# Second layers three turns behind, one split a turn, stores issued later on the sync queue, and the last two half slots under a condition

## The chip, the cores and the metric

The kernel runs on one core of a Trainium2 chip. Its engines work side by side, each in the order of its own instructions: PE (matmuls, with PEld for its weight loads), DVE and ACT (elementwise work; both read PSUM), POOL (small elementwise work, gathers and scatters) and SP, which here only issues DMAs; a DMA at the head of SP's queue that must wait holds all that stand behind it. The metric is the device time of one execution in microseconds (us), the median over runs.

## The reference

```python
X = np.fft.rfft(x, axis=1); y = np.fft.irfft(X * (filt_r + 1j * filt_i), n=3072, axis=1)   # x: 8 x 3072 x 256
h = y.reshape(24576, 256) @ w_in                      # 24576 x 1024
sm = softmax(h); solu = h * sm
ln = (solu - mean) / sqrt(var + 1e-6) * g_ln
z = ln @ w_out                                        # 24576 x 256
logits = cosine(z, expert_emb) / tau                  # 8 experts
e = argmax(logits); gate = softmax(logits)[e]
out = gate * (relu(z @ w1[e]) @ w2[e])                # one expert for each token
```

## The kernel before

The length 3072 is split as 64 x 48, and the transforms become matmuls. Four pairs of batches are worked on, p = 0 to 3. `fft(p)` has two passes: `stage1` loads the input, multiplies and stores to the DRAM tensor `bufA`; the second pass loads `bufA`, transforms over 48, applies the filter and stores to `bufC`. `inv4` takes the last inverse step from `bufC` and leaves tokens, split in two float16 parts (`xh`, L715 and L716), as weights for the first layer.

**Stage B** (`stage_b`) has 192 turns, one for 128 tokens (48 for each p). In turn i PE does the first layer of tile i + 1 (`mm1`, L728, PSUM tile `h`, two buffers), DVE its maximum (`nm`, L893), ACT the exponent (`es`, L929), DVE the product (L930). The second layer (`o`, 24 matmuls, L945) needs `es` transposed and split in a high and a low float16 part, `T`. There are two ways to it. `turn` (L899 to 908) transposes on PE into the tile's `h`, then ACT and DVE split (L907, L908), and only then is that `h` buffer free. `send` (L910 to 917) splits in SBUF (ACT L914, DVE L915, tile `hl`) and lets a DMA of the sync queue transpose (L917). Up to turn 144 the even tiles go by `turn` and the odd ones by `send`; both stand in the odd turn i: `turn(i - 1)` at its start, `send(i)` after the second layer's matmuls. The even turn has neither. The second layer runs LAG = 2 turns behind. `b_final` works out experts, gates and places of each group of 8 tiles, some steps a turn.

Between these pieces `aux` advances the transforms of the next pair (and, for p = 3, the split of the experts' weights, `w_split`), so that in turns 0 to 143 they fill the same engines; their PSUM tiles and inv4's are `a`, two buffers in turn. DMAs on SP stand where the code emits them: the stores of `bufA` (L516) and `bufC` (L679) right behind the ACT instruction that fills their source, the filter load `ft` (L555) inside the first half of a step, the stores of token rows to `xs` (L978) right behind DVE's L974.

**Stage C** (`stage_c`) runs the experts over slots of tokens of one expert: 24 slots of 256 made early, 65 more of 256, and `rest` = 21 half slots of 128, a number that holds for any routing:

```python
full = -(-(n - E * (BLK - 1)) // BLK)          # 89 for n = 24576
rest = (n - full * BLK - E) // 128 + E         # 21
```

A half slot gathers its rows (L1121), has them transposed by DMA (L1126), does 48 matmuls of the first layer (L1197) and 24 of the second (L1160) and scatters 128 rows to `out` (L164). Half slots beyond the last token have ids out of bounds: they do all this and write nothing. The loop is straight code; the instruction stream has no branch in it.

Of the kernel before, what the change touches and what calls it, by code (L numbers as in the profile page):

```python
# [33 lines left out]
LAG = 2  # L34
# [4 lines left out]
WAIT = 4  # L39
MAGIC = 0x5F3759DF  # L40
# [112 lines left out]
class Build:  # L153
    def __init__(self, tc, a, np_run=NP):
        self.tc, self.nc, self.a = tc, tc.nc, a
        self.np_run = np_run
        self.scattered = {}
        self.ld1 = {}
        self.later = []

# [248 lines left out]
    def w_max(self, sp, ps):  # L409
# [5 lines left out]
        for t in range(64 + 2):  # L415
# [81 lines left out]
    def stage1(self, p, part, ap, ps, bufA):  # L497
# [5 lines left out]
        for c in range(n):  # L503
# [5 lines left out]
            for j in range(0, CH, b):  # L509
# [3 lines left out]
                nc.scalar.activation(ao[:, j:j + b, :], t, AF.Copy)  # L513
                yield
            for h in range(2):
                (nc.sync if p else nc.scalar).dma_start(bufA[part, h, c * CH:(c + 1) * CH, :, :].rearrange("n k d -> k n d"), ao[h * 64:(h + 1) * 64])  # L516
# [7 lines left out]
    def fft(self, p, ap, ps, hp):  # L524
# [71 lines left out]
        if p > 0:  # L596
            yield
            yield
            yield
# [16 lines left out]
        for j in range(n + 2):  # L616
            steps = filt(j - 1) if 1 <= j <= n else iter(())
            next(steps, 0)
            if j < n:
# [9 lines left out]
                for i in range(0, KC, b):  # L629
# [8 lines left out]
                    if i == 0:  # L638
                        load2(j + (4 if p > 0 else 2))
                        load_f(j + 2)  # L640
# [16 lines left out]
            for _ in steps:  # L657
                pass
            if j >= n:
                self.load1(p + 1, j - n, ap)  # L660
            if j >= 2:
# [3 lines left out]
                for i in range(0, KC, b):  # L665
# [8 lines left out]
                    nc.scalar.activation(co[:, i:i + b, :], t[:96], AF.Copy)  # L674
                    next(other, 0)
                    yield
                nc.scalar.activation(y[-1], co, AF.Square, accum_out=self.csq[:, p, j - 2:j - 1])
                for h in range(2):
                    (nc.sync if p else nc.scalar).dma_start(bufC[h, first(j - 2):first(j - 2) + KC, :, cols(j - 2)].rearrange("k n d -> n k d"), co[h * 48:(h + 1) * 48])  # L679

        if p > 0:
            yield
            yield
# [56 lines left out]
    def b_final(self, t, p, n2, gw, ps, snap, slow):  # L740
# [74 lines left out]
        if not slow:  # L815
            v.tensor_reduce(gate, pe, axis=AX.X, op=ALU.add)
        yield 2
# [39 lines left out]
    def stage_b(self, xp, bps, gp, ps, hp, op, aux, early):  # L857
# [18 lines left out]
        rows, half = None, None  # L876
# [33 lines left out]
        def send(i):  # L910
# [4 lines left out]
            nc.vector.tensor_tensor(hl[:, 1, :], M["s"], hl[:, 0, :], op=ALU.subtract)  # L915
            T = M["T"] = M["pool"].tile([128, 16, 128], F16, name="T", tag="T")
# [4 lines left out]
        for i in range(n + LAG):  # L921
            j = i - LAG
            now = 0 <= i < n
            if 0 <= i - 1 < n and i != n - 1 and (i % 2 or i > n - N2):
                turn(i - 1)
# [23 lines left out]
            if now:  # L949
                if i % 2 and i < n - N2:  # L950
                    send(i)
# [12 lines left out]
            if now:  # L964
                aux(*divmod(i, N2), 1)
            if 0 <= j < n:
# [4 lines left out]
                def half(j=j, k=k, o=o, c2=c2, rows=rows):  # L971
# [3 lines left out]
                    if k % 2 == 1:  # L975
# [15 lines left out]
        if half:  # L991
            half()
        while finals:
# [14 lines left out]
    def table(self, sp, tp, ps, nb, start, K, blk, out):  # L1008
# [20 lines left out]
        out["taken"] = taken  # L1029
        yield  # L1030
# [64 lines left out]
    def other_slots(self, sp, tp, ps):  # L1095
# [16 lines left out]
        yield from self.table(sp, tp, ps, nb, x2, rest, 128, {})  # L1112
# [16 lines left out]
    def stage_c(self, cb, hp, op, ps, side):  # L1129

        nc = self.nc
        wt = {}

        def load(s):
            while s >= len(self.tables):
                if next(side, 1) == 1:
                    return
            for _ in self.load_slot(s, cb):
# [28 lines left out]

        weights(0, 0)
# [3 lines left out]
        s = 0  # L1172
        late = None
        while s in self.loaded:
            load(s + 2)
            xT = self.loaded.pop(s)
            tab, k = self.tables[s]
            w1, w2 = wt[s]
            n = tab["nh"] * 128
            w1 = w1.rearrange("p (l k f) -> p l k f", l=2, k=2)  # L1180
            w2 = w2.rearrange("p (l k f) -> p l k f", l=2, k=8)
            m = 512 // n
            fs = 1024 // n
            hh, hl = [], []
            for j in range(8 // m):
                if j == 8 // m - 2:
                    weights(s + 1, 0)
                if m * j % fs == 0:
                    hh.append(cb.tile([128, fs, n], F16, name="chh", tag="chh", bufs=2))
                    hl.append(cb.tile([128, fs, n], F16, name="chl", tag="chl", bufs=2))  # L1190
                t = (ps.tile([128, m, n], F32, name="a", tag="a") if j % 2 else hp.tile([128, m, n], F32, name="h", tag="h"))
                for i in range(m):
                    f = m * j + i
                    q = 0
                    for db in range(2):
                        for l, r in ((0, 0), (1, 0), (0, 2)):
                            nc.tensor.matmul(t[:, i, :], w1[:, l, db, f * 128:(f + 1) * 128], xT[:, r + db, :n], start=q == 0, stop=q == 5)  # L1197
                            q += 1
                sl = slice(m * j % fs, m * j % fs + m)
                nc.scalar.activation(hh[-1][:, sl, :], t, AF.Relu)  # L1200
                nc.vector.scalar_tensor_tensor(hl[-1][:, sl, :], t, 0.0, hh[-1][:, sl, :], op0=ALU.max, op1=ALU.subtract)  # L1201
                next(side, 0)
            if late:
                second(late)
            weights(s + 1, 1)
# [148 lines left out]
```

## Time and profile before

| | |
|---|---|
| median of 3 runs | 2778.83 us (2777.41 to 2781.04) |
| the profiled execution | 2770.33 us, its span 2768.5 us, mean granted clock 0.983 |
| first transform alone | 0 to 179 us |
| stage B | 179 to 1698 us |
| stage C | 1698 us to the end |

The page's slices show PE at nine tenths or more nearly everywhere after the first. Matmuls are pipelined and the page models their ends, so a busy PE can hide short gaps; an idle time of a microsecond or more is real. The DMA engines are at seven to nine tenths up to about 1300 us and at three tenths in stage C.

### The profile page before, as it was taken

How to read it: one execution, taken by the hardware profiler on the slowest of the kernel's cores; microseconds unless marked ns; L12 is line 12 of the kernel's file. 1: busy time of each engine (PE TensorE's matmuls, PEld its weight loads, DVE VectorE, ACT ScalarE, POOL GpSimd, SP SyncE). 2: the span in 40 equal slices, each digit the busy share in tenths (PEclk: the TensorE clock that was granted, in tenths of full speed). 3: DMA queues.
4: the chain of work that ended last, by engine and by line, in shares of the span. 5: the costliest groups of instructions: out<-in, count | busy, mean ns of one | idle time of the engine just before them, and what ended most of it. 6: DMA issues, size and time to landing. Idle time of an engine off the chain costs nothing.

```text
span 2768.5 us, 53941 instructions
## 1 busy us (share of the span) xinstructions
PE 2642.6 (95%) x20234; PEld 2035.6 (74%) x20234; DVE 1897.8 (69%) x2976; ACT 1529.8 (55%) x2858; POOL 1245.2 (45%) x2633
## 2 busy tenths in 40 slices
PE   6889999999999998999999998999999999999998
PEld 5447666666666675666677777888888888888898
DVE  5846888867898768988788985554544545545465
ACT  3556777767777766877788864323333333333332
POOL 2001245434555444554455556744454444544444
PEclk8999999999999999999999999999999999999999
DMA  9868888799787798876444432332222333223222
GB/s 316 221 178 248 196 209 185 186 218 211 178 196 181 204 231 201 187 172 140 104 123 121 120 72 50 78 77 73 77 77 75 78 75 78 76 75 79 75 59 57
DMA packets 445398, 384.66 MB, mean 139 GB/s; under 512 B 285995, under 2 KB 368053, under 8 KB 442064
## 3 DMA queue, kind: packets, MB, share of 16 engines
q1 hardware_dynamic: 392288, 310.60, 46.6%
q0 software_dynamic: 27088, 57.48, 6.8%
q10 hardware_dynamic: 25760, 13.14, 1.8%
q8 instruction: 159, 2.61, 0.4%
q14 instruction: 103, 0.84, 0.1%
HBM read 195.93 MB, written 103.35 MB: 108 GB/s over the span
## 4 chain that ended last, share of the span: by engine, by line
PE 30%; issue 23%; POOL 19%; DVE 14%; DMA 8%; ACT 4%; SPq 1%; POOLq 0%; ACTq 0%; DVEq 0%
PE h L728 10%; PE o L945 9%; POOL crow L1121 7%; POOL out_dram L164 6%; POOL scr L163 3%; DVE nm L893 3%; DVE es L930 2%; PE a L512 2%; PE h L904 2%; PE a L667 2%; PE a L710 2%; DMA bufA<-out 2%; DMA c<-bufC 1%; DVE T L908 1%; ACT hl L914 1%
## 5 line engine op out<-in xcount | busy, mean ns | idle before, releaser
L945 PE MATMUL o<-wo_h,T 128*128 128x264 f16 x3072 | 552.8, 277 | 3.3 <-DMA T<-hl 3.2
L1160 PE MATMUL o<-cw,chh 128*128 128x256 f16 x3184 | 527.6, 273 | 0.0
L728 PE MATMUL h<-win_h,xh 128*128 128x512 f16 x1536 | 497.3, 385 | 25.8 <-DVE T L908 22.5
L1197 PEld LDWEIGHTS <-cw 128*128 128x128 f16 x5280 | 476.1, 98 | 57.3 <-POOL gu L761 6.5
L945 PEld LDWEIGHTS <-T 128*128 128x128 f16 x4608 | 452.4, 98 | 70.0 <-DMA T<-hl 3.6
L896 POOL TENSOR_SCALAR gcc<-nm 128x1 f32<-128x1 f32 x192 | 118.6, 618 | 813.3 <-DVE nm L894 533.6
L728 PEld LDWEIGHTS <-xh 128*128 128x128 f16 x2304 | 223.6, 99 | 310.3 <-issue 81.2
L1160 PE MATMUL o<-cw,chl 128*128 128x256 f16 x1592 | 434.0, 273 | 3.0 <-DVE chl L1201 3.0
L945 PE MATMUL o<-wo_l,T 128*128 128x264 f16 x1536 | 425.5, 277 | 0.0
L164 POOL DMA_INDIRECT out_dram<-cot,ids x199 | 218.4, 1097 | 454.8 <-ACT cot L1163 443.0
L1201 DVE SCALAR_TENSOR_TENSOR chl<-h,chh 128x512 f16<-128x512 f32 x199 | 135.8, 683 | 392.1 <-ACT chh L1200 392.1
L1160 PEld LDWEIGHTS <-chh 128*128 128x128 f16 x3184 | 310.6, 98 | 35.5
L1163 ACT ACTIVATE cot<-o,fac 128x256 f32<-128x256 f32 x199 | 94.5, 475 | 423.8 <-PE o L1160 421.8
L1149 DVE COPY cw<-wexp 128x4096 f16 x220 | 279.9, 1280 | 44.3 <-PE o L1160 23.6
L893 DVE TENSOR_REDUCE nm<-h 128x1 f32<-128x1024 f32 x192 | 234.0, 1219 | 105.5 <-PE h L728 105.3
L1197 PE MATMUL h<-cxT,cw 128*128 128x256 f16 (+1 forms) x2640 | 295.1, 263 | 6.8 <-POOL gu L761 6.2
L728 PE MATMUL h<-win_l,xh 128*128 128x512 f16 x768 | 295.9, 385 | 0.0
L1197 PE MATMUL a<-cxT,cw 128*128 128x256 f16 (+1 forms) x2640 | 294.0, 262 | 0.0
L930 DVE SCALAR_TENSOR_TENSOR es<-h,gcc,es 128x1024 f32<-128x1024 f32 x192 | 245.6, 1279 | 65.3 <-ACT es L929 49.4
L929 ACT ACTIVATE es<-h,nm,isc_h 128x1024 f32<-128x1024 f32 x192 | 230.7, 1201 | 61.6 <-DVE nm L894 46.0
L1121 POOL DMA_INDIRECT crow<-xs,ids x199 | 203.5, 1022 | 65.8 <-issue 63.8
L164 POOL DMA_INDIRECT lst<-gdi,gix x192 | 209.1, 1089 | 35.1 <-issue 32.9
(262 smaller groups left out, 4355.9 us busy)
## 6 DMA issues: line engine op xcount, KB each, us to landing
wst<-in_w_dram SPq DMA_DIRECT2D x128, 256.0 KB
in<-in_x_dram SPq DMA_DIRECT2D x48, 512.0 KB
in<-bufA SPq DMA_DIRECT2D x64, 384.0 KB
c<-bufC SPq DMA_DIRECT2D x96, 256.0 KB
xs<-rows SPq DMA_DIRECT2D x96, 256.0 KB
ft<-in_filt_dram SPq DMA_DIRECT2D x24, 960.0 KB
bufA<-out SPq DMA_DIRECT2D x72, 256.0 KB
zw<-z SPq DMA_DIRECT2D x96, 192.0 KB
```

The costliest lines, as they stand in the source:

```text
L164: ins = self.nc.gpsimd.indirect_dma_start(in_offset=None, **kw).ins
L728: nc.tensor.matmul(h[:, nb, :], l[:, i, db, :], r[:, db, sl], start=k == 0, stop=k == 5)
L893: nc.vector.tensor_reduce(x[:, 0:1], L["h"], axis=AX.X, op=ALU.max, negate=True)
L896: nc.gpsimd.tensor_scalar(cc, nm, nm, 1.0, op0=ALU.mult, op1=ALU.max)
L929: nc.scalar.activation(L["s"], L["h"], AF.Exp, bias=L["nm"], scale=self.isc_h[:, i // N2:i // N2 + 1], accum_out=col(i, "st", 0))
L930: nc.vector.scalar_tensor_tensor(L["s"], L["h"], col(i, "cc", 0), L["s"], op0=ALU.mult, op1=ALU.mult, accum_out=col(i, "st", 1))
L945: nc.tensor.matmul(o[:, :D + E], T[:, l, :], r[:, f, :], start=q == 0, stop=q == 23)
L1121: nc.gpsimd.indirect_dma_start(out=rows[:, h, :], out_offset=None, in_=self.xs, in_offset=bass.IndirectOffsetOnAxis(ap=tab["ids"][:, h, k: ...
L1149: nc.vector.tensor_copy(w.rearrange("p (o k) -> p o k", o=1), self.wexp[:, bass.ds(e, 1), part * 4096:(part + 1) * 4096])
L1160: nc.tensor.matmul(o[:, :D], l[f // fs][:, f % fs, h * 128:(h + 1) * 128], w2[:, r, f, :], start=q == 0, stop=q == 23)
L1197: nc.tensor.matmul(t[:, i, :], w1[:, l, db, f * 128:(f + 1) * 128], xT[:, r + db, :n], start=q == 0, stop=q == 5)
L1201: nc.vector.scalar_tensor_tensor(hl[-1][:, sl, :], t, 0.0, hh[-1][:, sl, :], op0=ALU.max, op1=ALU.subtract)
```

## The change

Seven edits in one:

- LAG goes from 2 to 3; `T` has four buffers.
- `send` is cut in two. The split (ACT and DVE) of the odd tile i - 1 stands at the start of the even turn i; the DMA transpose (`post`) follows in that turn behind the second layer's matmuls.
- The stores to `bufA` and `bufC` on the sync queue (p > 0) are held and issued after a later ACT copy (`flush`); the store of token rows (`puts`) is issued at the end of the turn.
- The filter load for p > 0 is issued after the step's filter work rather than in its middle.
- The reduction of `w_max` is emitted one step earlier.
- In the slow form of `b_final` a step is one turn longer.
- The number of half slots in use is read into a register of every engine, and the last two half slots stand in a branch that is taken only if more than 19 are used. The slot loop becomes the function `slots`.

Two tiles that held constants for the first transform move to another pool.

```diff
-LAG = 2
+LAG = 3
+SPARE = 2
@@ w_max
-            yield
             if t >= 2:
                 nc.vector.tensor_reduce(acc[:, (t - 2) // 32, ...
+            yield
@@ stage1 (the same with bufC in fft, where j - 2 is bound too)
                 nc.scalar.activation(ao[:, j:j + b, :], t, AF.Copy)
+                self.flush()
                 yield
-            for h in range(2):
-                (nc.sync if p else nc.scalar).dma_start(bufA[part, h, ...
+            def put(c=c, ao=ao):
+                for h in range(2):
+                    (nc.sync if p else nc.scalar).dma_start(bufA[part, h, ...
+            if p:
+                self.held.append(put)
+            else:
+                put()
+    def flush(self):
+        for f in self.held:
+            f()
+        self.held.clear()
@@ fft
                     if i == 0:
+                        self.flush()
                         load2(j + (4 if p > 0 else 2))
-                        load_f(j + 2)
+                        if p == 0:
+                            load_f(j + 2)
...
             for _ in steps:
                 pass
+            if p > 0:
+                load_f(j + 2)
@@ b_final, after goh
         if not slow:
             v.tensor_reduce(gate, pe, axis=AX.X, op=ALU.add)
+        else:
+            yield
@@ stage_b
+            M["hl"] = hl
+        def post(i):
+            M = live[i]
+            hl = M["hl"]
             T = M["T"] = M["pool"].tile([128, 16, 128], F16, name="T", tag="T")
             nc.sync.dma_start_transpose(out=T, in_=hl.rearrange("p a b -> p (a b)"))
...
-            if 0 <= i - 1 < n and i != n - 1 and (i % 2 or i > n - N2):
-                turn(i - 1)
+            if 0 <= i - 1 < n and i != n - 1:
+                (turn if i % 2 or i > n - N2 else send)(i - 1)
...
             if now:
-                if i % 2 and i < n - N2:
-                    send(i)
+                if 0 < i <= n - N2 and i % 2 == 0:
+                    post(i - 1)
...
                 aux(*divmod(i, N2), 1)
+            if puts:
+                puts.pop()()
...
-                    if k % 2 == 1:
+                    def put():
                         ...
                         nc.sync.dma_start(to[:, nn:nn + 2, :], rows)
+                    if k % 2 == 1:
+                        puts.append(put)
...
-            if i >= n - N2 + SPLIT + 2:
+            if i >= n - N2 + SPLIT + LAG:
                 next(early, 0)
@@ table
+        used = out["used"] = tp.tile([1, 1], I32, name=f"used{len(self.tables)}")
+        v.tensor_copy(used, src[0:1, E - 1:E])
@@ stage_c (the loop over slots is now slots(s), its body as before)
+        stop[0] = end - SPARE                     # load(s) returns for s >= stop[0]
         weights(0, 0)
         next(side)
         load(1)
         weights(0, 1)
+        slots(0)
+        used = nc.values_load(self.used[0:1, 0:1], min_val=0, max_val=end)
+        with tc.If(used > rest - SPARE):
+            stop[0] = end
+            for s in range(end - SPARE, end):
+                load(s)
+            weights(end - SPARE, 0)
+            weights(end - SPARE, 1)
+            slots(end - SPARE)
@@ run
-            bps[0] = ... {"nm": 2, "es": 2, "jk": 1, "hl": 2, "T": 3}
+            bps[0] = ... {"nm": 2, "es": 2, "jk": 1, "hl": 2, "T": 4}
-                    self.m1 += [pp.tile([128, 4, 128], F32, name=f"m1_{k}") for k in range(2)]
+                    self.m1 += [ap.tile([128, 4, 128], F32, name="mt", tag="mt", bufs=3) for _ in range(2)]
```

DVE, in a pair of turns of a second pass. `T` is the split of `turn`, `hl` that of `send`, `es` the product, `xh` inv4's low part, `nm` the maximum of the next tile, `in`, `zw` and `y` the transform. Before, an odd turn and the start of the even one:

```order
L908 TENSOR_TENSOR T<-h,T 128x1024
L930 SCALAR_TENSOR_TENSOR es,gst<-h,gcc,es 128x1024
L974 SCALAR_TENSOR_TENSOR rows<-o,gcc,rows 128x256
L915 TENSOR_TENSOR hl<-es,hl 128x1024
L893 TENSOR_REDUCE nm<-h 128x1
L894 TENSOR_SCALAR nm<-nm,isc_h 128x1
L584 TENSOR_TENSOR y<-z,ft 96x1024
L422 TENSOR_REDUCE wm_a<-wst 128x1
L967 COPY graw<-o 128x8
L792 RECIPROCAL grn<-gnrm 128x8
L930 SCALAR_TENSOR_TENSOR es,gst<-h,gcc,es 128x1024
L716 SCALAR_TENSOR_TENSOR xh<-a,ysc,xh 128x512
```

The same place after the change:

```order
L940 TENSOR_TENSOR T<-h,T 128x1024
L968 SCALAR_TENSOR_TENSOR es,gst<-h,gcc,es 128x1024
L1014 SCALAR_TENSOR_TENSOR rows<-o,gcc,rows 128x256
L925 TENSOR_REDUCE nm<-h 128x1
L926 TENSOR_SCALAR nm<-nm,isc_h 128x1
L600 TENSOR_TENSOR y<-z,ft 96x1024
L423 TENSOR_REDUCE wm_a<-wst 128x1
L1007 COPY graw<-o 128x8
L947 TENSOR_TENSOR hl<-es,hl 128x1024
L968 SCALAR_TENSOR_TENSOR es,gst<-h,gcc,es 128x1024
L746 SCALAR_TENSOR_TENSOR xh<-a,ysc,xh 128x512
```

`hl` has left the place ahead of the maximum `nm` in the odd turn and stands ahead of `es` and `xh` in the even one.

SP, some turns of the same pass. Before:

```order
L650 DMA zw<-z 48x1024
L651 DMA zw<-z 48x1024
L917 DMA_TRANSPOSE T<-hl 128x16x128
L679 DMA bufC<-out 48x4x256 x2
L561 DMA in<-bufA 96x1024
L555 DMA ft<-in_filt_dram 96x2560
L418 DMA wst<-in_w_dram 128x512
L697 DMA mt_8065<-in_m_dram 128x256
L699 DMA c_8067<-bufC 128x512
L978 DMA xs<-rows 128x512
```

After:

```order
L1018 DMA xs<-rows 128x512
L727 DMA mt_8026<-in_m_dram 128x256
L729 DMA c_8028<-bufC 128x512
L955 DMA_TRANSPOSE T<-hl 128x16x128
L669 DMA zw<-z 48x1024
L670 DMA zw<-z 48x1024
L571 DMA ft<-in_filt_dram 96x2560
L703 DMA bufC<-out 48x4x256 x2
L577 DMA in<-bufA 96x1024
L420 DMA wst<-in_w_dram 128x512
```

The transpose stood ahead of the loads of inv4 (`mt`, `c`); it now follows them, and the row store stands ahead of them.

POOL, the end of the program after the change; before, the scatters of `out` run on to the last instruction:

```order
L165 MEMSET scr 1x1
L166 DMA out_dram<-cot,ids_22010 24576x256
L1274 TENSOR_LOAD used_21658
L1275 COMPARE_AND_BRANCH
L1169 DMA crow<-xs,ids_22010 128x256 x2
L165 MEMSET scr 1x1
L166 DMA out_dram<-cot,ids_22010 24576x256
L165 MEMSET scr 1x1
L166 DMA out_dram<-cot,ids_22010 24576x256
L1275 UNCONDITIONAL_BRANCH
L1275 ISA
L1275 UNCONDITIONAL_BRANCH
```

The two half slots stand behind the compare, and the ISA row belongs to the path that leaves them out.

## Rows read from the trace of the kernel before

**Rows 1.** Busy time by stretch: stretch, length, engines' busy time (instructions), clock, DMA share, GB/s.

```profile
700.00:900.00 200.00, 192.13 (x1210) 126.13 (x1210) 181.34 (x284) 155.27 (x294) 106.97 (x255) 0.99 0.81 186
...
179.00:1698.00 1519.00, 1457.66 (x9623) 1006.70 (x9623) 1241.88 (x2122) 1115.73 (x2122) 693.89 (x1920) 0.99 0.71 171
```

**Rows 2.** PE's waits from 179 to 1330: us in total, times, longest.

```profile
PE h L728 <- DVE T L908: 16.5, 10, 3.7
PE a L710 <- DMA c<-bufC: 6.7, 4, 3.0
PE a L633 <- DVE xh L716: 4.9, 3, 1.9
PE a L512 <- DVE xh L716: 3.9, 2, 2.0
PE a L667 <- DVE xh L716: 3.5, 5, 1.4
...
PE o L945 <- DMA T<-hl: 3.2, 2, 2.8
PE a L512 <- ACT hl L914: 2.0, 1, 2.0
```

**Rows 3.** PE's waits from 1330 to 1698.

```profile
PE h L728 <- DVE T L908: 6.0, 6, 1.3
```

**Rows 4.** POOL in order of time, the end: start, us, instruction, idle before.

```profile
2740.64 1.73 POOL L164 DMA_INDIRECT out_dram<-cot,ids  x1 [2.20 <-ACT cot L1163]
...
2745.93 1.73 POOL L164 DMA_INDIRECT out_dram<-cot,ids  x1 [2.20 <-ACT cot L1163]
...
2759.57 0.98 POOL L164 DMA_INDIRECT out_dram<-cot,ids  x1 [1.61 <-ACT cot L1163]
```

**Rows 5.** POOL's DMA queue, 2751.4 to 2756.7 and from 2756.7: packets, MB.

```profile
q0 software_dynamic: 48, 0.04, 2.5%
...
q0 software_dynamic: 96, 0.00, 0.5%
```

**Rows 6.** Lines L1147 and L1350: instructions, ns min/median/max, first and last start.

```profile
L1147 DVEq TENSOR_LOAD <-er x220: 299/307/707, 1698.7 to 2748.9; - x110
...
L1350 POOLq DRAIN  x3: 46/103/8405, 2759.3 to 2768.3; - x3
```

**Rows 7.** DMA queues: an instruction queue; scatters, median us from issue to landing.

```profile
q8 instruction: 159, 2.61, 0.4%
...
out_dram<-cot,ids POOLq DMA_INDIRECT x199, 2.5
```

**Rows 8.** DVE by line, 179 to 1698: busy us, mean ns, idle before.

```profile
L915 DVE TENSOR_TENSOR hl<-es,hl 128x1024 f16<-128x1024 f32 x72 | 88.1, 1223 | 43.3 <-ACT hl L914 43.3
```

**Rows 9.** SP's waits from 179 to 1330.

```profile
SPq L917 <- DVE hl L915: 308.2, 56, 9.9
...
SPq L555 <- DVE zw L590: 49.9, 11, 7.1
```

**Rows 10.** SP and PE in order of time around 1040.

```profile
1035.99 0.95 SPq L555 DMA_DIRECT2D ft<-in_filt_dram  x1
...
1047.03 1.27 PE L710 MATMUL a<-mt,c 128*128 128x128 f32 x8 [2.95 <-DMA c<-bufC]
```

**Rows 11.** DVE and PE in order of time, an even turn.

```profile
1081.95 0.74 DVE L716 SCALAR_TENSOR_TENSOR xh<-a,ysc,xh 128x512 f16<-128x512 f32 x1
...
1084.16 0.58 PE L633 MATMUL a<-hi,d2h 96*96 96x512 f32 x1
```

**Rows 12.** Busy time by stretch behind three gaps of PE.

```profile
391.50:396.00 4.50, 4.33 (x24) 3.08 (x25) 3.92 (x6) 1.62 (x3) 0.28 (x2) 0.62 1.01 345
...
1047.50:1051.50 4.00, 4.00 (x23) 2.95 (x23) 3.25 (x5) 3.68 (x7) 1.31 (x4) 0.57 1.22 218
...
1093.30:1099.50 6.20, 6.17 (x14) 2.38 (x14) 5.89 (x7) 3.30 (x7) 4.85 (x9) 0.53 0.60 132
```

**Rows 13.** The chain that ended last, in order of time.

```profile
197.12 2.70 PE o L945 x24
```

More of the change, by code (lines that the diff above doesn't have):

```diff
@@ L677, in fft, with put @@
                 nc.scalar.activation(y[-1], co, AF.Square, accum_out=self.csq[:, p, j - 2:j - 1])
[L678 to L679 removed]
+                def put(j=j - 2, co=co):
+                    for h in range(2):
+                        (nc.sync if p else nc.scalar).dma_start(bufC[h, first(j):first(j) + KC, :, cols(j)].rearrange("k n d -> n k d"), co[h * 48:(h + 1) * 48])
+                if p:
+                    self.held.append(put)
+                else:
+                    put()
         if p > 0:
             yield
+            self.flush()
             yield
@@ L875, in stage_b @@
         xs = [next(src)]
-        rows, half = None, None
+        rows, half, puts = None, None, []
         def begin(i):
@@ L992, in stage_b @@
             half()
+            puts.pop()()
         while finals:
@@ L1111, in other_slots @@
         yield
-        yield from self.table(sp, tp, ps, nb, x2, rest, 128, {})
+        t2 = {}
+        yield from self.table(sp, tp, ps, nb, x2, rest, 128, t2)
+        self.used = t2["used"]
     def load_slot(self, s, pool):
@@ L1137, in load @@
                     return
+            if stop[0] is not None and s >= stop[0]:
+                return
             for _ in self.load_slot(s, cb):
@@ L1166, in second, with slots @@
                 next(side, 0)
+        def slots(s):
+            late = None
+            while s in self.loaded:
+                load(s + 2)
+                xT = self.loaded.pop(s)
+                tab, k = self.tables[s]
+                w1, w2 = wt[s]
+                n = tab["nh"] * 128
+                w1 = w1.rearrange("p (l k f) -> p l k f", l=2, k=2)
+                w2 = w2.rearrange("p (l k f) -> p l k f", l=2, k=8)
+                m = 512 // n
+                fs = 1024 // n
+                hh, hl = [], []
+                for j in range(8 // m):
+                    if j == 8 // m - 2:
+                        weights(s + 1, 0)
+                    if m * j % fs == 0:
+                        hh.append(cb.tile([128, fs, n], F16, name="chh", tag="chh", bufs=2))
+                        hl.append(cb.tile([128, fs, n], F16, name="chl", tag="chl", bufs=2))
+                    t = (ps.tile([128, m, n], F32, name="a", tag="a") if j % 2 else hp.tile([128, m, n], F32, name="h", tag="h"))
+                    for i in range(m):
+                        f = m * j + i
+                        q = 0
+                        for db in range(2):
+                            for l, r in ((0, 0), (1, 0), (0, 2)):
+                                nc.tensor.matmul(t[:, i, :], w1[:, l, db, f * 128:(f + 1) * 128], xT[:, r + db, :n], start=q == 0, stop=q == 5)
+                                q += 1
+                    sl = slice(m * j % fs, m * j % fs + m)
+                    nc.scalar.activation(hh[-1][:, sl, :], t, AF.Relu)
+                    nc.vector.scalar_tensor_tensor(hl[-1][:, sl, :], t, 0.0, hh[-1][:, sl, :], op0=ALU.max, op1=ALU.subtract)
+                    next(side, 0)
+                if late:
+                    second(late)
+                weights(s + 1, 1)
+                late = (tab, k, w2, hh, hl, fs)
+                if tab["nh"] > 1:
+                    second(late)
+                    late = None
+                wt.pop(s)
+                s += 1
+            if late:
+                second(late)
+        n = self.np_run * 2 * S
+        full = -(-(n - E * (BLK - 1)) // BLK)
+        rest = (n - full * BLK - E) // 128 + E
+        end = full + rest
+        stop[0] = end - SPARE
         weights(0, 0)
@@ L1171, in stage_c @@
         weights(0, 1)
[L1172 to L1205, printed above, removed]
-            late = (tab, k, w2, hh, hl, fs)
-            if tab["nh"] > 1:
-                second(late)
-                late = None
-            wt.pop(s)
-            s += 1
-        if late:
-            second(late)
+        slots(0)
+        assert len(self.tables) == end
+        used = nc.values_load(self.used[0:1, 0:1], min_val=0, max_val=end)
[6 more added lines that the diff above has]
+            slots(end - SPARE)
     def run(self):
```

13 lines of the change are left out of this document (9 added, 4 removed).

## The prediction

> **What bounds the kernel now.** I read the busy times by stretch first, then who PE waited for, then SP's waits, then the last twenty microseconds engine by engine. The stretches [rows 1] should show two regimes. Stage B is 1519.00 us long and PE is busy in 1457.66 of them, so 61.3 us at most are idle; in 700 to 900, where the transforms' second pass fills DVE too, PE has 192.13 of 200 and DVE 181.34. So B is bound by PE with DVE close behind, and no reordering can give more than the idle 61 us plus what the lower clock costs. Stage C has PE without a gap, and only work left out can shorten it.
>
> The waits of PE tell what the 61 us are. Up to turn 144 [rows 2] the largest is the first layer waiting for DVE's T (the buffer `h` that `turn` must leave): 16.5 us in 10 waits. Then come loads from DRAM, `c` 6.7 us, the PSUM buffer `a` that DVE's `xh` must free (4.9 + 3.9 + 3.5 = 12.3 us), the transposed T by DMA 3.2 us, and ACT's `hl` 2.0 us. In the last 48 turns [rows 3], where all tiles go by `turn`, 6.0 us of waits for T are left; nothing of the change moves the split there.
>
> **The two half slots.** Near the end the scatters come 5.29 us apart [rows 4]: that is one half slot, first layer, second layer and no gap. Are the last two in use? The last scatters moved 0.00 MB in 96 packets, and the one before them 0.04 MB in 48 [rows 5]. So 19 of 21 half slots hold tokens; the condition asks for more than 19, and the branch is not taken. The slots end in the same pattern as before (first layer, the second layer of the slot before, the own second layer), two earlier: -2 x 5.29 = -10.6 us, with no cover to lose, since PE is the bound there.
>
> What the condition adds stands at the end of each engine's queue, and POOL is the last. It loads a register: 0.307 us, the median of DVE's loads of an expert's number [rows 6]. Then it waits for its scatters to land, 2.5 us after the issue [rows 7], before the drain may start; before, the drain of 8.405 us began at 2759.3 while the last scatter was still to be issued. From below the cost is the register load, +0.3 us. From above the drain starts at 2759.57 + 2.5 + 0.3 = 2762.4, 3.1 us late. No row shows a compare. I take +2.0, nearer the late drain, since the order puts the wait ahead of it; nothing else is queued there.
> The Trainium skill (Runtime: NRT & Kernel Launch, Instruction fetch mechanics) says that a taken branch whose target is outside the pages held forces a fetch by DMA before the engine goes on. What such a fetch would cost is in the trace: 159 instruction packets take 0.4% of 16 engines' 2768.5 us, 1.1 us each [rows 7]. No run here shows a branch in the stream; that case is a rival below.
>
> **The split in two.** The instructions stay 72 on ACT and 72 on DVE at 1223 ns [rows 8]; they change place. Before, SP stood at the transpose with 308.2 us of waits for DVE's `hl` in 56 turns, the longest 9.9 us, and what was queued behind it (row stores, `in`, `ft`, `c`) waited along; at `ft` it stood another 49.9 us for the filter's `zw` [rows 9]. After, the transpose is issued when its source has been split for most of a turn, and `ft` after its wait is over. I cost SP's freedom only by the waits of PE that it can end.
> - T by DMA: issued earlier in its turn and read as many turns later, it has landed. -3.2 us (bounds 0 and -3.2).
> - `c`: one of the long waits has `ft` issued at 1035.99, the load behind it, and PE idle for 2.95 us before L710 starts at 1047.03 [rows 10]. Here the filter load is a pass's first, which the change leaves where it is, but the held stores ahead of it no longer keep it late. Half of 6.7: -3 us (bounds 0 and -6.7).
> - T by `turn`, 16.5 us: in the odd turn DVE has 1.22 us less to do ahead of the maximum, so the next exponent, and with it the next `es`, comes earlier. In the even turn it has 1.22 us more ahead of `xh` and of everything up to the next T. DVE's sum over the pair is the same, and at nine tenths it leaves little slack. I take a third, -5 us; bounds -16.5 and, where the even turn's delay reaches T, the third rival's price.
> - ACT's `hl`, which held an `a` tile for 2.0 us behind the product that it waited for, now has its source ready at the turn's start: -2.0 us (bounds 0 and -2.0).
> - `a` freed by `xh`: 0. In the turn shown `xh` ends at 1082.69 and PE comes for the third `a` at 1084.16 [rows 11]: 1.47 us of slack, 0.25 after a delay of 1.22.
>
> **The clock.** After such gaps the granted clock falls to its lower level, 1.2 of 2.4 GHz, for a while: 0.62, 0.57 and 0.53 in three stretches with 4.33, 4.00 and 6.17 us of PE work [rows 12]. At full clock these 14.5 us would take little over half; all three gone would be -7 us, and I take -4, the first and half of the others (bounds 0 and -7).
>
> **One turn more of lag.** The 192 second layers stay; one moves from turn 2 to a turn behind the last first layer. There it lies bare: 2.70 us [rows 13]. At the start turn 2 lacks those 2.70 us, but its end is set by the chain through ACT and DVE, which the matmuls had covered in part. Between 0 and +2.7: +1.5 us. The step that `b_final` gains, the earlier reduction and the copy of the count lie on DVE and POOL beside PE's work and are taken at 0, a few tenths a group if DVE has no room.
>
> **The sum.** -10.6 + 2.0 - 3.2 - 3 - 5 - 2 - 4 + 1.5 = -24.3 us. The profiled execution took 2770.33 us, 1.83 more than its span, and would come to 2746.0. The median of the timed runs is 8.50 us above it; what is saved is work and waits, not a share, so I carry the difference: 2778.83 - 24.3 = 2754.5 us.
>
> **The rivals.**
> - Stage C alone: SP's waits go, but PE's are set by DVE and by transfers that compete for the DMA engines whatever the order. For it: DVE at 181.34 of 200, and half of `c`'s waits lie where `ft` is under way. Against it: the T by DMA waits on nothing else. -10.6 + 2.0 + 1.5 = -7.1: 2771.7 us.
> - All of it: the odd turn's relief frees T in time everywhere, and the clock holds. -10.6 + 0.3 - 3.2 - 6.7 - 16.5 - 2 - 7 + 0 = -45.7: 2733 us. Against it: DVE has the same sum to do.
> - The other side, slower: the even turn is DVE's heavier one, and `hl` ahead of `es` and `xh` delays both. The waits at `a` (12.3 us in 10 places) show where that slack is already gone. Without the gains at T by `turn`, the rest is -10.6 + 2.0 + 1.5 - 3.2 - 3 - 2 - 2 = -17.3; it decides from 17.3 / 1.22 = 14 even turns that pay the whole 1.22. Of the 72 even turns up to 144, 10 wait now; half of the other 62 would pay 31 x 1.22 = 37.8: +20.5, 2799 us. Against it: the 1.47 us of slack, and the maximum that comes earlier by what `hl` gives up.
> - The branch costs more: POOL jumps twice, into the path that leaves the slots out and out of it, and each time waits for its instructions, 1.1 us by the packets above; with the full 3.1 for the drain instead of 2.0 that is +3.3 on the forecast: 2758 us. For it: the two half slots' instructions lie between. Against it: POOL has few there. The Trainium skill's section just named is the rule behind this one.
> - That it doesn't leave the slots out: the count would have to be 20 or 21, against the empty scatters. Then the two gathers start only inside the branch and the 10.6 us come back with their latency: 2754.5 + 10.6 + 8 = 2773 us.
>
> **Chances.** The forecast, with its own range 2744 to 2765, 0.52; all of it 0.11; stage C alone 0.20; the other side 0.07; the branch 0.08; the slots not left out 0.02. A measurement here can tell 0.2%, 5.6 us, from no change: faster means below 2773.3. Of stage C alone (1.6 us from that line) I count 0.14 as faster and 0.06 as the same; the unskipped slots lie on the line, 0.01 each way; of the other side 0.01 ends as the same. Faster 0.52 + 0.11 + 0.14 + 0.08 + 0.01 = 0.86, same 0.06 + 0.01 + 0.01 = 0.08, slower 0.06. The range for 8 in 10 reaches to both neighbours: 2735 to 2772.
>
> **What would show it.** Scatters in stage C: 197 instead of 199, the last at about 5.29 x 2 us less after stage B's end, and the last drain's end no more than 3 us late against the last scatter. SP's waits for `hl` near zero, and no wait of PE for T by DMA. PE idle in B near 45 us and the stretches of lower clock fewer. The forecast is wrong if PE's waits for DVE's T or for `xh` grow beyond 35 us together, if B is no shorter, or if the time between the last scatter and the end grows by more than 4 us.

## The result

| | before | changed |
|---|---|---|
| median | 2778.36 us (2777.41 to 2781.04, 4 runs) | 2746.88 us (2744.74 to 2749.49, 4 runs) |
| ratio | | 0.9888 (0.9872 to 0.9904) |
| profiled execution | 2770.33 us | 2744.74 us |

On a second chip the changed kernel had the ratio 0.9893 (0.9874 to 0.9912). The median fell by 31.5 us where 24.3 were forecast (2754.5 us, range 2735 to 2772); between the two profiled executions it is 25.6, since before's lay 8.0 us under its median and the changed kernel's 2.1.

The stretches, cut at PE's first first-layer matmul, at the first of stage C and at PE's last. First the two of the changed kernel: stretch, length, busy time of PE, PEld, DVE, ACT and POOL, clock, DMA share, GB/s.

```profile
186.57:1683.67 1497.10, 1442.26 (x9624) 1005.38 (x9625) 1245.16 (x2128) 1117.90 (x2124) 786.55 (x1930) 0.99 0.74 175
1683.67:2731.26 1047.59, 1040.28 (x9937) 932.53 (x9937) 538.38 (x683) 328.53 (x591) 525.20 (x656) 1.00 0.29 74
```

The same cuts in the kernel before:

```profile
179.12:1703.95 1524.83, 1457.66 (x9623) 1006.72 (x9624) 1245.20 (x2127) 1116.83 (x2124) 699.00 (x1929) 0.99 0.71 171
1703.95:2758.73 1054.78, 1049.09 (x10081) 943.04 (x10081) 544.47 (x689) 331.89 (x597) 530.30 (x662) 1.00 0.29 75
```

The first transform took 186.57 us against 179.12, stage B 27.73 less, stage C 7.19 less, the end (2742.87 - 2731.26 = 11.61 against 9.81) 1.80 more. In stage B the same matmuls keep PE busy 15.4 us less, most of it because they ran less at the lower clock: 15.7 us of the stage against 40.0. PE's idle time fell from 67.2 to 54.8 us. The first transform's instructions stand in the same order in both; its length differs from run to run (below).

PE's waits of the changed kernel from 186.57 to 1683.67: us in total, times, longest.

```profile
PE h L758 <- DVE T L940: 33.5, 33, 2.9
PE h L1245 <- DMA cxT<-crow: 7.1, 1, 7.1
PE a L650 <- DVE xh L746: 4.4, 4, 2.1
PE a L514 <- DVE xh L746: 3.6, 3, 1.6
PE a L688 <- DVE xh L746: 3.1, 3, 1.2
PE h L936 <- DVE es L968: 2.3, 2, 1.4
```

Against [rows 2, 3] every wait within the stage for a load, for T by DMA and for `hl` is gone, those for `xh` stand nearly as they were (11.1 us against 12.3), and the one for T by `turn` has grown from 22.5 to 33.5 us. The 7.1 us for `cxT` are the wait at the first matmul of stage C. Before, that place has one too, put down to another engine:

```profile
PE h L1197 <- POOL gu L761: 6.2, 1, 6.2
```

What SP waits for, 186 to 1330 us:

```profile
SPq L955 <- DVE hl L947: 144.5, 41, 5.2
SPq L1018 <- DVE rows L1014: 99.5, 33, 7.0
```

Against [rows 9] the waits for `hl` have halved. But SP is not free: all its waits from 179 to 1330 us together are 656 us against 673. It stands at the transpose for 339 us instead of 473 and at the filter load for 16 instead of 55, and in their place at the row stores (109 instead of 45) and at the stores to `bufC` (88 instead of 9).

The end: POOL's last scatter (start, us, instruction), the branch's line and the drain's (instructions, ns min/median/max, first and last start).

```profile
2732.09 0.98 POOL L166 DMA_INDIRECT out_dram<-cot,ids  x1 [1.61 <-ACT cot L1215]
```

```profile
L1275 POOLq COMPARE_BRANCH  x1: 54/54/54, 2732.8 to 2732.8; - x1
L1275 POOLq INC_SWDGE_SEM  x1: 1861/1861/1861, 2733.3 to 2733.3; - x1
```

```profile
L1418 POOLq DRAIN  x3: 46/103/6852, 2735.2 to 2742.6; - x3
```

The drain starts 3.1 us behind the start of the last scatter instead of ahead of it [rows 4, 6]. Of these, 1.86 are a semaphore instruction on the path that leaves the slots out. The drain is 1.55 us shorter.

### The profile page after: what moved, and what is told of

The parts are those of the page before. It is cut to its first block, busy times and chain, and to the rows that moved or that the text cites. A ratio compares the mean times of both kernels' runs of the same rounds, so it can differ in the third digit from the quotient of the medians.

```text
span 2742.9 us, 53684 instructions
## 1 busy us (share of the span) xinstructions
PE 2620.9 (96%) x20090; PEld 2024.3 (74%) x20090; DVE 1891.5 (69%) x2971; ACT 1527.3 (56%) x2852; POOL 1328.7 (48%) x2627
## 4 chain that ended last, share of the span: by engine, by line
PE 39%; issue 23%; POOL 20%; DVE 12%; DMA 4%; ACT 1%; POOLq 0%; SPq 0%; ACTq 0%; DVEq 0%
PE h L758 15%; PE o L983 11%; POOL crow L1169 7%; POOL out_dram L166 6%; POOL scr L165 3%; DVE nm L925 3%; PE a L514 2%; PE a L688 2%; PE h L936 2%; PE a L740 2%; POOL gcc L928 2%; DMA bufA<-out 1%; DVE T L940 1%; DVE in L586 1%; PE a L650 1%
## 5 line engine op out<-in xcount | busy, mean ns | idle before, releaser
L928 POOL TENSOR_SCALAR gcc<-nm 128x1 f32<-128x1 f32 x192 | 180.3, 939 | 725.3 <-DVE nm L926 485.7
L758 PE MATMUL h<-win_h,xh 128*128 128x512 f16 x1536 | 492.4, 382 | 35.1 <-DVE T L940 33.5
L1201 DVE COPY cw<-wexp 128x4096 f16 x216 | 275.2, 1281 | 41.1 <-PE o L1212 20.7
L995 ACT ACTIVATE jk<-es 128x1024 bf16<-128x1024 f32 x192 | 202.1, 1052 | 64.2 <-DVE es L968 63.0
L166 POOL DMA_INDIRECT lst<-gdi,gix x192 | 218.1, 1136 | 35.3 <-issue 33.0
```

Source lines behind the costliest of these rows:

```text
L166: ins = self.nc.gpsimd.indirect_dma_start(in_offset=None, **kw).ins
L758: nc.tensor.matmul(h[:, nb, :], l[:, i, db, :], r[:, db, sl], start=k == 0, stop=k == 5)
L928: nc.gpsimd.tensor_scalar(cc, nm, nm, 1.0, op0=ALU.mult, op1=ALU.max)
L995: nc.scalar.activation(jk, L["s"], AF.Square, accum_out=col(i, "st", 2))
L1201: nc.vector.tensor_copy(w.rearrange("p (o k) -> p o k", o=1), self.wexp[:, bass.ds(e, 1), part * 4096:(part + 1) * 4096])
```

## The experiments

Ratios are to runs of the kernel before on the same chip at the same time (2767.7 us in runs 1 to 4, 2774.2 in runs 5 to 8 on that chip later, 2772.3 in runs 9 to 12 on another), lengths from each run's one profiled execution, in us: the first transform, stage B, stage C and the end, cut as above.

| | ratio (95%) | transform | B | C | end |
|---|---|---|---|---|---|
| before | | 179.1 | 1524.8 | 1054.8 | 9.8 |
| changed | 0.9888 (0.9872 to 0.9904) | 186.6 | 1497.1 | 1047.6 | 11.6 |
| 1 condition alone | 0.9963 (0.9947 to 0.9978) | 178.5 | 1514.9 | 1044.0 | 11.6 |
| 2 stores and filter load alone | 0.9996 (0.9986 to 1.0005) | 177.7 | 1522.3 | 1056.8 | 9.8 |
| 3 changed without these | 0.9921 (0.9907 to 0.9935) | 180.4 | 1508.8 | 1043.9 | 11.6 |
| 4 group's step behind T | 0.9843 (0.9829 to 0.9856) | 176.1 | 1483.7 | 1046.5 | 11.7 |
| 5 changed, again | 0.9893 (0.9874 to 0.9912) | 181.2 | 1500.6 | 1047.4 | 11.6 |
| 6 changed, lag two | 1.0076 (1.0054 to 1.0098) | 186.5 | 1548.0 | 1047.5 | 11.6 |
| 7 as 4, raw copy behind T | 0.9950 (0.9931 to 0.9970) | 180.6 | 1517.1 | 1052.6 | 11.7 |
| 8 as 4, split behind `xh` | 0.9835 (0.9815 to 0.9855) | 187.0 | 1482.2 | 1050.2 | 11.7 |
| 9 lag three alone | 1.0017 (1.0002 to 1.0032) | 176.7 | 1530.4 | 1061.1 | 9.8 |
| 10 as 4, positions behind T | 0.9884 (0.9861 to 0.9906) | 181.3 | 1499.5 | 1050.4 | 11.7 |
| 11 as 10, split behind `xh` | 0.9904 (0.9877 to 0.9930) | 186.3 | 1499.2 | 1050.7 | 11.7 |
| 12 as 4, again | 0.9830 (0.9807 to 0.9853) | 181.9 | 1484.6 | 1047.8 | 11.7 |

The first transform's instructions stand in the same order everywhere: its 176 to 187 us are a spread between executions, and the 7.45 us by which it was longer in the changed kernel's profile are not the change's. Stage B with before's code took 1524.8 and 1514.9 us (run 1): 10 us of one profile are no evidence.

**1. The condition alone**

```diff
+        with tc.If(used > rest - SPARE):
...
+            slots(end - SPARE)
```

> The kernel before with the conditional last two half slots and nothing else of the change. My theory: two half slots of 5.29 us go from the end of stage C (-10.6 us) and the time from PE's last matmul to the end of the span grows by 1.8 us (9.81 to 11.61 in the profile of the changed kernel); nothing else moves: -8.8 us, 2769.6 us, ratio 0.9968, first layer of stage C to its last matmul 1044.2 us against 1054.8. Rival: the branch, or the code behind it, also costs the 3.4 us that stage C of the changed kernel lost in its first slots (one 14.95 us against 13.03): -5.4 us, 2773.0 us, and the early slots show that loss again. Stage A is the same code as before: 179 us if the 7.5 us that it took longer in the changed kernel's profile are the change's, anything from 177 to 188 if stage A differs from run to run.

Measured -10.2 us by the ratio (-14.7 to -6.1), which holds the theory's -8.8 and not the rival's -5.4; stage C -10.8, the end +1.83. The early slots are as before (13.10 us for the one named, 261.8 against 261.5 for all 24), so what they lost in the changed kernel's profile (264.8) is not the condition's.

**2. The sync queue's part alone**, and **3. the changed kernel without it**

Run 2 puts this part of the change into the kernel before; run 3 takes it out of the changed kernel:

```diff
# 3
-            if p:
-                self.held.append(put)
-            else:
-                put()
+            put()
...
-                        if p == 0:
-                            load_f(j + 2)
+                        load_f(j + 2)
...
-            if p > 0:
-                load_f(j + 2)
```

> The kernel before with the sync queue's part of the change alone: stores of out, co and rows held until a later point, the filter load behind its wait; the split in two stays in one piece in the odd turn, lag two, no condition. Theory that stage B's gain comes from the split's move (SP no longer stands at the transpose): the loads stay stuck behind the 308 us that SP waits for hl; -4 us at most, 2774 to 2779 us, PE's waits for c and for the 128x128 mt load near 10 us, the granted clock lower in as many stretches as before (10 between the first layer's start and stage C). Rival, that the held stores free the loads: waits for c, mt gone (-10 us) and half the stretches of lower clock with them (-6): about -16 us, 2762 us.

> The changed kernel with its stores issued at once and the filter load in its old place again; split in two pieces, lag three and condition stay. If the split's move alone frees SP: 2747 us, within 3 us, of the changed kernel, waits for T by DMA and for hl at zero, SP's waits for hl well under 308 us. Rival, that the held stores make the gain: waits of PE for c and for mt come back (10 us) and with them the stretches of lower clock, 2757 to 2763 us.

Run 2: no difference, as the theory had it. SP stands at the transpose as before:

```profile
SPq L946 <- DVE hl L944: 337.0, 58, 10.0
```

Waits for `c` did shrink, to 1.7 us, but those for T by DMA rose to 7.4. Run 3 has most of the gain, against its rival; PE's waits for `c` are 0.5 us in it. What its theory had at zero and is left without the held stores is

```profile
PE o L974 <- DMA T<-hl: 9.6, 6, 2.3
```

which in runs of the changed kernel is 0. So holding the stores alone is worth nothing; with the split moved it ends these waits, and what that is worth in time is not shown clear of noise (0.9921 against 0.9893, with intervals that overlap, against runs of the kernel before at two times that differ by 6.5 us).

**6. Lag two**, and **9. lag three alone**

```diff
# 6, against the changed kernel
-LAG = 3
+LAG = 2
# 9, against the kernel before (T with four buffers as well)
-LAG = 2
+LAG = 3
```

> The changed kernel with its second layers two turns behind again; the split stays in two pieces, posted in the even turn. My theory, that the third turn of lag is what the transposed T needs to land in time (posted in the even turn, read in the next): PE waits for T by DMA in many of the 72 odd turns, 0.5 to 1 us each, 30 to 70 us together, and the time is 2775 to 2815 us where the changed kernel has 2746. Rival, that the posting's place alone matters and T lands within a turn: no such waits, and the bare second layer at the end (2.7 us) is gone: 2743 us.

> The kernel before with its second layers three turns behind and nothing else: the split stays in one piece in the odd turn, stores at once, no condition. What is open is which part of the split's change shortens stage B, since the early posting with two turns of lag alone is slower than before (ratio 1.0076). Theory: lag and place belong together. Lag alone takes PE's waits for T by DMA away (3.2 us) and some of the loss to the clock, but SP still stands over 300 us at the transpose, and PE's waits for c and mt stay: 2 to 5 us faster than before, ratio 0.998 to 1.000. Rival: the lag is the whole gain, and the place only shifts waits: ratio about 0.993 (the changed kernel's 0.9893 without the 0.0037 of the condition), PE's idle time in stage B 12 us less.

Each half of the split's change without the other is slower than before: run 6 by 0.76%, though the condition and the held stores are in it, run 9 by 0.17%, just clear of noise. Run 6 fell into its theory's range; run 9 missed its theory, which had it 2 to 5 us faster. Run 6, PE's waits in stage B:

```profile
PE o L983 <- DMA T<-hl: 60.1, 42, 5.8
PE h L758 <- DVE T L940: 6.6, 8, 1.7
```

Run 9, PE's waits, 179 to 1330 us, and below them SP's:

```profile
PE a L710 <- DMA c<-bufC: 13.2, 6, 4.0
PE h L728 <- DVE T L908: 11.9, 6, 4.1
```

```profile
SPq L978 <- DVE rows L974: 260.0, 65, 10.3
SPq L917 <- DVE hl L915: 97.7, 59, 1.9
```

With lag alone SP stands at the row store for most of what it no longer stands at the transpose. How early a transfer was issued tells the rest. From the end of SP's issue to PE's first matmul on what it brought, us, median and lowest tenth (`c` from 200 to 1330 us, T over all):

| | `c` | T by DMA |
|---|---|---|
| before | 10.2, 7.2 | 7.1, 5.1 |
| 9 lag three alone | 10.3, 8.0 | 15.6, 13.3 |
| 6 early post, lag two | 18.3, 15.1 | 3.3, 2.4 |
| 3 both, stores at once | 13.4, 8.7 | 9.4, 3.7 |
| changed | 15.9, 13.1 | 11.0, 8.6 |

A transpose lands 5.6 us after the start of its issue (median, run 4, 400 to 1300 us), 3.4 us after the end of it:

```profile
T<-hl SPq DMA_TRANSPOSE x57, 5.6
```

With lag two the issue ends 3.3 us ahead of the use, about what the landing takes, and in 42 of 72 turns PE waits. With lag three alone `c` is issued no earlier than before. Only both together bring both in time. The early post with lag two and nothing else was not run.

**5. The changed kernel again**

> The changed kernel once more, so that it stands beside the others on one chip. If the other chip's ratio of 0.9888 is the change's: 0.9888 again, within 0.002, and stage A anywhere from 176 to 187 us. If a part of that ratio was the chip's: 0.992, the ratio of the kernel without held stores (0.9921).

The ratio came again, 0.9893, and the transform took 181.2 us. Waits for T by `turn` 31.5 us in 30 places, for T by DMA none.

**4 and 12. The group's step behind T**

```diff
+            if i % 2:                       # behind turn(i - 1) and es
+                finals = [(f, x) for f, x in ((f, next(f, 1)) for f, _ in finals) if x != 1]
...
-            finals = [(f, x) for f, x in ((f, next(f, 1)) for f, _ in finals) if x != 1]
+            if i % 2:
+                finals = [(f, x) for f, x in ((f, next(f, 1)) for f, _ in finals) if x != 1]
```

> The changed kernel with one move on DVE: in front of each odd turn the step of the group's end (a few DVE instructions of 0.1 to 0.2 us each) is put behind T's second half and es instead of ahead of them. Theory: PE's waits at the first layer for T, 33.5 us in 33 places, which lie in three of four odd turns (13.5 and 13.3 us in the two of eight turns where most of those steps stand), are DVE's row, a microsecond late: with the step behind T they fall to 15 us or less, and the kernel gains 12 to 18 us: about 2732 us. Rival: DVE is full in those turns (its sum decides, not the order), so the wait comes back at xh, y or es, and the time stays at 2747 us.

> The kernel with the group's step behind T once more, on the chip of the two that build on it: ratio 0.984 to the kernel before, within 0.002, and a stage B (first layer's start to stage C) of 1484 us within 5.

DVE in order of time in an odd turn of the changed kernel, where PE waits 1.37 us for T:

```profile
745.54 1.21 DVE L608 TENSOR_TENSOR y<-y,zw 96x1024 f32<-96x1024 f32 x1
746.67 0.16 DVE L1007 COPY graw<-o 128x8 f32<-128x8 f32 x1
746.75 0.21 DVE L840 SCALAR_TENSOR_TENSOR gd<-gd,cst 128x64 f32<-128x64 f32 x1
746.99 0.22 DVE L842 TENSOR_REDUCE go<-gd 128x8 f32<-128x64 f32 x1
747.25 0.23 DVE L843 TENSOR_TENSOR goh<-gd,go 128x64 f16<-128x64 f32 x1
747.39 0.20 DVE L802 RECIPROCAL grc<-gcc 128x8 f32<-128x8 f32 x1
747.50 0.12 DVE L803 TENSOR_SCALAR gy<-gV 128x16 int32<-128x16 int32 x1
747.53 1.22 DVE L940 TENSOR_TENSOR T<-h,T 128x1024 f16<-128x1024 f32 x1
```

The same turn in run 4:

```profile
733.96 1.21 DVE L608 TENSOR_TENSOR y<-y,zw 96x1024 f32<-96x1024 f32 x1
735.09 0.15 DVE L1009 COPY graw<-o 128x8 f32<-128x8 f32 x1
735.16 1.21 DVE L940 TENSOR_TENSOR T<-h,T 128x1024 f16<-128x1024 f32 x1
```

T ends 0.8 us earlier against `y`, and PE waits 0.57. Over stage B:

```profile
PE h L758 <- DVE T L940: 20.2, 22, 2.6
```

-13.3 us of this wait, those for `xh` (11.9) unchanged, stage B 13 to 17 us shorter than in the two profiles of the changed kernel, about -16 us by the ratios: with run 8 the best version, and run 12 gave it again. DVE's work is the same, so these 13.3 us came from the order in front of T; the 20.2 that are left did not go with it.

**7, 10, 8, 11. More of the same, and what stopped it**

```diff
# 7
-                nc.vector.tensor_copy(g["raw"][:, k, :], o[:, D:D + E])   # even turn, ahead of T
+                        nc.vector.tensor_copy(g["raw"][:, k, :], o[:, D:D + E])   # in half(), ahead of ACT's row
# 10
+            if i % 2:                                                     # behind half()
+                finals = [(f, next(f) if x == 3 else x) for f, x in finals]
+                finals = [(f, x) for f, x in ((f, next(f, 1)) for f, _ in finals) if x != 1]
# 8 and 11
-                (turn if i % 2 or i > n - N2 else send)(i - 1)
+                    send(i - 1)                                           # behind xs.append(next(src))
```

> The kernel with the group's steps behind T (2724.8 us) with one more DVE instruction taken from in front of T in every odd turn: the copy of the raw scores, 0.15 us, now stands behind T and es. Theory (DVE's order in front of T sets the 20.2 us in 22 places that are left there): each of the 22 gets 0.15 us shorter, and those below 0.15 go: -3 to -4 us, 2721 us. Rival, that DVE's sum sets it: no difference within 2 us, or waits for xh that grow by as much.

> The kernel with the group's step behind T, es (ratio 0.9843): now also the step that reads the positions out of PSUM (five DVE instructions, 1.0 us) waits in even turns until the odd turn has issued T, es and its half of the row. In the trace of that kernel those five stand in front of T at every wait of the turns 8k (0.7 to 1.1 us each, 7.8 us in all). Theory: these waits go, -6 to -9 us, ratio 0.981. Rival: as with the raw copy, ACT's row waits for DVE's reading of the same PSUM buffer, or the later steps meet the first layer: no change or slower, 0.984 to 0.995.

> The kernel with the group's steps behind T (2724.8 us), and in the even turn the split's two instructions moved behind es and xh. By my rival of the prediction (hl ahead of es and xh makes the even turn heavier) the waits of PE for xh, 11.9 us in 10 places, and for es, 2.5, get 1.2 us shorter each: -8 to -12 us, 2714 us. If xh is late for another reason there (the kernel before the change has the same 12.3 us in 10 places with no split in front of xh): no change, 2725 us, and SP's waits for hl grow from 144 us.

> The last kernel with the split in two also behind es and xh in the even turn (alone that gave 0.9835 where 0.9843 stood without it, waits for xh 5.2 us against 11.9). Theory: the two are independent, ratio 0.980. Rival: the split behind xh makes the transpose and its T later by what it saves at xh: 0.981, the same as without.

Run 7 lost 30 us against run 4: ACT's row now waits for the copy behind T and `es`, and PE's waits rose to 25.5 us for T and to 20.7 for `xh`. ACT's waits, 340 to 1330 us:

```profile
ACT rows L1018 <- DVE graw L1016: 125.4, 56, 4.9
```

Run 10 cleared the wait ahead of the tiles named (7.8 to 1.4 us), but ahead of tiles 2 of eight it rose from 6.0 to 11.0 and the waits for `xh` doubled:

```profile
PE a L650 <- DVE xh L746: 10.4, 8, 2.8
PE a L688 <- DVE xh L746: 10.2, 9, 1.6
```

Run 8 took the waits for `xh` from 11.9 to 5.4 us and the time did not move (0.9835 against 0.9843); added to run 10 (run 11) it brought T's waits to 31.6. The theories' numbers failed in all four. Run 8 went by its rival, SP's waits for `hl` at 229.7 us included, and run 10 fell into its rival's range; runs 7 and 11 were slower than either of theirs. In these runs there was room behind T for one step, not for two; why `xh` and T then come late in other turns was not followed further.

## Why the prediction was right, and where it was not

The direction and the range held; the fall was larger than forecast, 31.5 us against 24.3. That the two profiles differ by 25.6, close to the sum, is luck: without the first transform's 7.45 us, which are not the change's, they differ by 33.1. Two terms of the sum were far off, on opposite sides.

- **The bound.** B by PE with 61 us idle, C by PE alone: right. PE's idle time up to the last second layer came to 47.8 us, against "near 45" (61.0 before; 56.4 in run 1, whose stage B is before's).
- **The half slots, -10.6 + 2.0.** Right: 197 scatters, -10.8 in stage C and +1.83 at the end in run 1; the end is 11.6 to 11.7 us in all profiles with the condition and 9.8 in all without. The reason given for the +2.0 was wrong in part: 1.86 us is the semaphore instruction, and the later drain is shorter. Stage C of the changed kernel fell by 7.2 only. Its 24 early slots took 264.8 us (run 5: 264.6) against 261.5 before, 261.8 in run 1 and 261.5 in run 3: some 3 us that the sum did not hold. Runs 2 (263.5) and 9 (266.6) lose there too, and why is open.
- **The branch's rival.** Fell: the comparison takes 0.05 us on POOL, and the instruction queue shows 159 packets, as before [rows 7]. The Trainium skill's fetch on a taken branch (Runtime: NRT & Kernel Launch, Instruction fetch mechanics) adds no packet that the trace shows here.
- **T by DMA -3.2, `hl` -2.0.** Right, both gone. But the transpose needs the third turn of lag for it (run 6), which the prediction priced only as a cost. That cost is there, and larger than the 1.5 taken: from the last first layer's end to the last second layer's, 14.5 us against 11.6.
- **`c`, -3.** Too small: all 6.7 went, and with them waits that the sum did not hold (the input's `mt` 3.4, ACT's `z` 2.8 and smaller ones). The way there was not SP's freedom: SP waits nearly as long in all as before. It is the order on SP, by which `c` is issued 15.9 us ahead of its use instead of 10.2.
- **T by `turn`, -5: the step that failed.** The wait grew by 11.0. The prediction reasoned on the 1.22 us of the split in either turn. What the runs show in its place is what else stands between the maximum and T. PE's idle time ahead of the first layers, summed by tile number, is 13.5, 6.8 and 13.3 us for tiles 0, 2 and 6 of eight, where before it was 1.3, 5.7 and 18.7. Up to turn 144 before, one step of the group's end, 1.1 us of DVE, stood in front of T, for tile 6 alone. In the changed kernel that step stands in front of T for tile 0 and another (0.9 us) for tile 6; for tiles 2 and 4 it is one instruction of 0.2 us. An odd turn ahead of such a tile 0, where PE waits 1.67 us:

```profile
762.54 1.21 DVE L608 TENSOR_TENSOR y<-y,zw 96x1024 f32<-96x1024 f32 x1
763.67 0.15 DVE L1007 COPY graw<-o 128x8 f32<-128x8 f32 x1
763.75 0.22 DVE L861 TENSOR_TENSOR gpos<-o,base 128x72 f32<-128x72 f32 x1
764.00 0.17 DVE L863 COPY base<-gpos 128x8 f32<-128x8 f32 x1
764.08 0.22 DVE L866 TENSOR_TENSOR gpos<-gpos,goh 128x64 f32<-128x64 f32 x1
764.34 0.22 DVE L868 TENSOR_REDUCE gdst<-gpos 128x8 f32<-128x64 f32 x1
764.47 0.21 DVE L870 TENSOR_REDUCE ggate<-gpe 128x8 f32<-128x64 f32 x1
765.06 0.20 DVE L874 RECIPROCAL grg<-ggate 128x8 f32<-128x8 f32 x1 [0.38 <-POOL ggate L871]
765.18 1.17 DVE L940 TENSOR_TENSOR T<-h,T 128x1024 f16<-128x1024 f32 x1
```

  The lag alone does not bring it there. In run 9, which has the lag and not the turn that `b_final`'s slow form gained, the same turn has no step in front of T, and the idle time ahead of tiles 0 is 1.4 us in all of stage B:

```profile
779.47 1.21 DVE L592 TENSOR_TENSOR y<-y,zw 96x1024 f32<-96x1024 f32 x1
780.60 0.15 DVE L967 COPY graw<-o 128x8 f32<-128x8 f32 x1
780.68 1.21 DVE L908 TENSOR_TENSOR T<-h,T 128x1024 f16<-128x1024 f32 x1
```

  So the step that `b_final` gains, which the prediction took at 0, belongs to this term; the gained turn by itself was not run. Runs 4 and 10 moved steps behind T: the idle time fell from 13.3 to 6.1 us ahead of tiles 6, and ahead of tiles 0 from 13.5 to 7.8 and then to 1.4.
- **The clock, -4.** Too small. From the first layer's start to the last second layer the granted clock is lower in 36 us before and in 12.5 after; at half rate that is 11.7 us of the 15.4 that PE was busy less. With run 1's stage B (24 us at the lower clock) against run 5's (16.6) it is 6.9 of busy time, 3.7 of them by the clock: the gain is there in both pairs, its size differs between executions. One of the three such stretches left in stage B (length, busy times, clock):

```profile
1066.10:1069.50 3.40, 3.33 (x8) 1.13 (x8) 3.40 (x6) 1.59 (x5) 0.00 (x0) 0.50 1.08 243
```

  It lies behind a wait of 2.9 us, as those of before did behind waits of 1.3 to 3.7 us [rows 12]; the clock is at 1.2 of 2.4 GHz in it. Not every such wait is followed by one: before, the clock did not fall behind a wait of 3.0 us at 657 us.
- **The point named as decisive** (waits for T and `xh` over 35 us together) was crossed, 44.6, and yet the time came out below the forecast: other waits had gone in the meantime. A limit on the sum of all waits would have been the right one; this one was before's own value, 34.8. Another sign failed as well: SP's waits for `hl`, forecast "near zero", are 144.5 us, and PE's waits went all the same.
- **The slower rival.** Its mechanism is seen, its price is not: PE waits for `xh` in as many places as before, and freeing it (run 8) did not move the time.

## What to carry to other kernels

A transfer posted earlier, a consumer one step later and a queue kept free for it can be one change in three pieces. Here the held stores alone measured 0, the later consumer alone a loss of 0.2%, and the earlier post without the later consumer a loss too; together they gave -0.7%. After a reordering, look at what now stands directly in front of the instruction that the bound engine waits for; a handful of 0.2 us instructions there cost about 16 us of 2745, and a step delayed by one turn can be what puts them there. Give a prediction's test as the sum of an engine's waits, not as one of them.

## What the runs showed of the hardware

POOL's first instruction on the new exponent, one value per partition, takes 0.3 us beside DVE's reductions and beside `T` (read from PSUM; three cases), but waits out DVE's operations on two SBUF inputs: in the changed kernel its median is 1.3 us beside `hl`, 1.2 beside the `y` that reads `y`, 1.9 beside `zw` and 2.4 beside the `y` that reads `z`. (These are sorted by the DVE operation that ran at its start.) Two turns of the changed kernel, POOL in order of time:

```profile
745.74 1.20 POOL L928 TENSOR_SCALAR gcc<-nm 128x1 f32<-128x1 f32 x1 [1.90 <-DVE nm L926]
...
753.18 2.99 POOL L928 TENSOR_SCALAR gcc<-nm 128x1 f32<-128x1 f32 x1 [4.06 <-DVE nm L926]
```

The second spans `y` and the moved `hl` on DVE, and also 0.6 us between them in which DVE ran a reduction of one input; why it did not end there is open. The mean of this instruction rose from 0.69 to 1.14 us between 340 and 1330 us, and DVE's `es`, which needs the result, waited 25.2 us for POOL against 5.7 before: a price of the split's new place that the prediction did not have (the mean is 0.71 us in run 9, with the lag alone, and 0.92 in run 6, with the new place). What PE lost by it is not shown. The Trainium skill (SBUF — State Buffer, SBUF: two separate sides) names this lock of a port pair for DVE operations with two SBUF inputs; the trace agrees where the instruction takes as long as one such operation, 1.2 us, and doesn't show why the longer one goes on between two of them.
